# Fused dilated-window attention and squared-ReLU feed-forward: the second part of batch 0's plain values is loaded as f32 by SyncE and cast by VectorE, where GpSimd loaded and cast it before

## The chip, the cores and the metric

The kernel runs on one core of one Trainium2 chip. The number that counts is the device time of one execution in microseconds (us), the median of three runs. TensorE does the matrix products, ScalarE the exponentials, logarithms and most copies out of PSUM, VectorE the masks, products and other copies. GpSimd issues nearly all loads, because its DMAs can change f32 into bf16 on the way; SyncE issues the stores, the transposing DMAs and a few loads that change no type.

## The reference

Attention with a window of 32 keys over 8 batches, 8 heads, 576 tokens and 64 dimensions of a head. The first four heads ("plain") look at the last 32 tokens, the other four ("dilated") at every fourth of the last 128. Its result, as 4608 rows of 512, goes through a feed-forward layer with 2048 hidden columns and a squared ReLU.

```python
mask_plain = (rel >= 0) & (rel < window)                                    # rel = query - key, window = 32
mask_dil = (rel >= 0) & (rel < window * dilation) & (rel % dilation == 0)   # dilation = 4
scores = np.where(masks, scale * np.matmul(q, k.transpose(0, 1, 3, 2)), -1e9)
attn = np.exp(scores - np.max(scores, axis=-1, keepdims=True))
attn = attn / (np.sum(attn, axis=-1, keepdims=True) + 1e-09)
attn_out = np.matmul(attn, v)                                               # (8, 8, 576, 64)
x = attn_out.transpose(0, 2, 1, 3).reshape(4608, 512)
h = np.maximum(x @ w_in, 0.0)                                               # w_in (512, 2048)
out = h * h @ w_out                                                         # w_out (2048, 512)
```

## The kernel before

The order of everything is written by hand. A string PROGRAM lists short codes; a bar stands for one group of feed-forward matrix products. Codes that begin with L and a batch number are loads (`i0` to `i3` are the four column pieces of w_in, `o0` to `o3` the four row pieces of w_out, `v1p` the plain values of part two). For batch 0 the codes are a letter, a pair of heads e (0 and 1 plain, 2 and 3 dilated) and a part: T transposes q and k, C copies them out, S scores, E exponentials, P the product with the values, D the row sums, L and X the reciprocal, M the product into xT. Part one is the first 256 tokens of a batch, part two the other 320.

```python
PROGRAM = (
    "L0:q001 L0:q023 L0:q101 L0:q123 L0:v0d L0:i0 L0:v1dr L0:i1 L0:v1p L0:i2 L0:i3 L0:o0 L0:o1 L0:o2 L0:o3 "
    "L1:q00123 z y L1:v0dp L1:q10123 L1:v1dpr w9 T00 C00a ...  h W3 S20 E20 W2 S30 E30 T01 C01v ... P00 P10 D00 D10 L00 ..."
    "C31v W4 S01 S11 X00 M00 E01 E11 P20 P30 D20 D30 L20 X20 M20 S21 S31 W2+31 E21 E31 | | P21 P31 D21 D31 L21 "
    "X21 M21 L31 X31 M31 | | P01 P11 D01 D11 L01 X01 M01 L11 X11 M11 | | | ... "
    # ... (the rest: batches 1 to 7)
)
```

The values of the plain heads stand in `vbd[0]`, one 128 by 128 block for each pair of heads and 64 keys, with one head's values in the upper left and the other's in the lower right quarter. GpSimd loads those of part two (keys 256 to 575, five blocks) straight into it, four DMAs of 64 partitions, f32 in memory and bf16 in the tile:

```python
            if what == "p":                       # load_v; L0:v1p comes here with i0 = 4, i1 = 9
                for e in range(NE // 2):
                    for hl, rows in sides:
                        nc.gpsimd.dma_start(
                            dst[rows, e, i0:i1, rows],
                            v[b, 2 * e + hl, 64 * i0 : 64 * i1, :].rearrange("(i p) d -> p i d", p=64),
                        )
```

Part one takes another way: SyncE and ScalarE load it as f32 into a buffer of the output pool, which no output needs so early, and VectorE casts it into `vbd[0]` (code h):

```python
    osb_pool = ctx.enter_context(tc.tile_pool(name="osb", bufs=3))
    # ...
    plain = osb_pool.tile([P, DM], f32, name="osb")[:, :].rearrange("p (e i d) -> p e i d", e=2, d=D)
    nc.vector.tensor_copy(plain[:, :, 0, 0:1], mk[:, 0:2].unsqueeze(2))      # the loads wait for this copy
    for e, engine in enumerate((nc.sync, nc.scalar)):
        for hl, rows in enumerate(sides):
            engine.dma_start(
                plain[rows, e, :, :], v[0, 2 * e + hl, 0:256, :].rearrange("(i p) d -> p i d", p=64)
            )
    # ...
        elif code == "h":
            for rows in sides:
                nc.vector.tensor_copy(vbd[0][rows, 0:2, 0:4, rows], plain[rows, :, :, :])
```

The product with the values (P01 and P11 are part two of the plain pairs; each reads block 3 of part one first, then blocks 4 to 8), the product into xT (M), and the weights' load:

```python
        elif what == "P":      # first_step
            # ...
            for x, (i, r, q0, q1) in enumerate(bl):          # e 0 and 1, part two: blocks 3, 4 to 8
                # ...
                    lhs = vbd[0][:, e, i, :]
                    nc.tensor.matmul(to, lhs, rhs, start=(x == 0 and y0 == 0), stop=(x == len(bl) - 1), ...)   # line 595
        # ...
                nc.vector.tensor_tensor(out=to, in0=o, in1=rec, op=ALU.mult)                                   # M, line 628

    def load_w_in(x):          # line 776
        nc.gpsimd.dma_start(w_in_sb[x][:, :, :], moe_w_in[:, w_cuts[x] : w_cuts[x + 1]].rearrange("(kt p) f -> p kt f", p=P))
```

DMAs are counted on eight semaphores for GpSimd's and eight for the others', taken in turn. A DMA is issued once the one that used its semaphore eight DMAs earlier has landed.

The feed-forward products of the first 512 tokens run as two tiles of 256. Line 676 is the product with w_in, line 687 the ReLU on ScalarE, line 688 the square on VectorE, line 711 the product with w_out. An output tile of 128 tokens is copied out of PSUM and stored; in the last 512 tokens each store is cut into two halves of 256 columns:

```python
            if f1 == NF:       # g2
                osb = osb_pool.tile([P, DM], f32, name="osb")
                # ...
                nc.scalar.copy(osb[:, c0:mid], cur[m][:, c0:mid])                                             # line 718
                # ...
                for x in (c0, DM // 2) if c1 - c0 == DM and tk0 == NTOK - NT else (c0,):
                    store(osb, tk0 + P * m, x, DM // 2 if x < min(c1, DM // 2) and tk0 == NTOK - NT else c1)
```

Of the kernel before, what the change touches and what calls it, by code (L numbers as in the profile page):

```python
# [18 lines left out]


PROGRAM = (  # L21
    "L0:q001 L0:q023 L0:q101 L0:q123 L0:v0d L0:i0 L0:v1dr L0:i1 L0:v1p L0:i2 L0:i3 L0:o0 L0:o1 L0:o2 L0:o3 "
    "L1:q00123 z y L1:v0dp L1:q10123 L1:v1dpr w9 T00 C00a T10 C10a B00 B10 W2 S00 E00 B20 W1 S10 E10 u B30 W3 "
    "T20q W6 T20k C20v T30 C30v h W3 S20 E20 W2 S30 E30 T01 C01v T11 C11a P00 P10 D00 D10 L00 T21 C21v T31 "
    "C31v W4 S01 S11 X00 M00 E01 E11 P20 P30 D20 D30 L20 X20 M20 S21 S31 W2+31 E21 E31 | | P21 P31 D21 D31 L21 "
    "X21 M21 L31 X31 M31 | | P01 P11 D01 D11 L01 X01 M01 L11 X11 M11 | | | | | | | | | | | | | m n | | | | | "
    "L2:q00123 L2:q10123 | 1q1 1q3 | 1q2f 1k2f | 1k1a 1v3 | 1a2 | 1v2 1k0a 1q0v | 1o2 | 1a0 1a1 | 1k3 1o0 1o1f "
    "| 1a3 1Q0 | 1K0 1o3 | 1Q1 1K1 | 1Q2 | 1b0 | | 1Q3 1K2 L2:vwpdr L3:q00123 L3:q10123 | L2:x | | 2q0 | | 2k0 "
    "1V2 | 1b2 1p0 | 1b1 1V3 1K3 | | 1p2 1p1f | 2a0 1b3 | 2k1l 2o0 1p3f 2b0 2k1h | 2q1 2k2 L3:x | | 2q2 2p0 "
# [34 lines left out]
def kernel(  # L64
# [9 lines left out]
    nc = tc.nc  # L74
    P = nc.NUM_PARTITIONS
    B, H, S, D = q.shape
    DM, DFF = moe_w_in.shape
    NTOK = B * S
    assert H * D == DM
    bf16 = mybir.dt.bfloat16  # L80
    f32 = mybir.dt.float32
# [5 lines left out]
    NB = S // 64  # L87
# [5 lines left out]
    NT = 512  # L93
# [15 lines left out]
    osb_pool = ctx.enter_context(tc.tile_pool(name="osb", bufs=3))  # L109
# [23 lines left out]
    xT = const.tile([P, KT, RING], bf16, name="xT")  # L133
# [9 lines left out]
    vbd = [const.tile([P, NE, NB, P], bf16, name=f"vbd{i}") for i in range(2)]  # L143
# [6 lines left out]
    def staged(b: int, nm: str):  # L150


        t = rb[STAGE[b]][nm]
        return t[:, :].rearrange("p (a h x) -> p a h x", h=H, a=2)
# [309 lines left out]
    sides = [slice(64 * hl, 64 * hl + 64) for hl in range(2)]  # L464
# [175 lines left out]
    def store(osb, pos: int, c0: int = 0, c1: int = DM):  # L640

        x = 0
        while x < P:
            b, y = divmod(pos + x, S)
            part = int(y >= RES * MN[0]) if b in PARTED else 0
            w = MN[part] if b in PARTED else M
            r, m = divmod(y - RES * MS[part], w)
            n = min(P - x, w - m)
            row = b * S + RES * (MS[part] + m) + r
            nc.sync.dma_start(out[row : row + RES * (n - 1) + 1 : RES, c0:c1], osb[x : x + n, c0:c1])  # L650
            x += n

    def ffn_groups(tk0: int, nt: int):

        early = NT <= tk0 <= 2 * NT
        h2 = h2_pool.tile([P, NF, NT], bf16, name="h2T")
        per = NT // nt
        kts = (0, 2, 1, 3) if tk0 >= NT else (0, 1, 2, 3) if tk0 == 0 else (2, 3, 0, 1)  # L660
        cut = 3 if tk0 >= NT else 2
        cur, acc = {}, {}

        cuts = [(0, nt)] if tk0 // RING == (tk0 + nt - 1) // RING else [(0, -tk0 % RING), (-tk0 % RING, nt)]

        def mm1(u, ks):
            if u not in acc:
                acc[u] = ps_f.tile([P, NT], f32, name="pf")
            for x in range(per):
                f = per * u + x  # L670
                piece = max(y for y in range(len(w_in_sb)) if w_cuts[y] <= P * f)
                c0 = 512 * (f // 4) + f % 4 - w_cuts[piece]
                for kt in ks:
                    for y0, y1 in cuts:
                        t0 = (tk0 + y0) % RING
                        nc.tensor.matmul(  # L676
                            acc[u][:, nt * x + y0 : nt * x + y1],
                            w_in_sb[piece][:, kt, c0 : c0 + 509 : 4],
                            xT[:, kt, t0 : t0 + y1 - y0],
                            start=(kt == kts[0] and x == 0 and y0 == 0),  # L680
                            stop=(kt == kts[-1] and x == per - 1 and y1 == nt),
                            skip_group_check=True,
                        )
            if ks[-1] != kts[-1]:
                return
            hv = h2[:, per * u : per * u + per, 0:nt]
            nc.scalar.activation(hv, acc[u][:, :].rearrange("p (x n) -> p x n", x=per), ACT.Relu)  # L687
            nc.vector.tensor_tensor(out=hv, in0=hv, in1=hv, op=ALU.mult)  # L688

        def g1(i):  # L690
            if i < 2 and tk0 < NT:
                for u in range(2):
                    mm1(u, kts[2 * i : 2 * i + 2])
            elif i < 2 and early:
                for u in (2 * i, 2 * i + 1):
                    mm1(u, kts[:cut])
            elif i < 4 and early:
                for u in (2 * i - 4, 2 * i - 3):
                    mm1(u, kts[cut:])
            else:  # L700
                mm1(i, kts)

        def g2(m, part):
            last = tk0 + P * (m + 1) == NTOK
            if part == 0 or last and part == 2:
                cur[m] = ps_f.tile([P, DM], f32, name="pf")

            c0, c1 = (DM // 2 * (part // 2), DM // 2 * (part // 2 + 1)) if last else (0, DM)
            f0, f1 = (NF // 2 * (part % 2), NF // 2 * (part % 2 + 1)) if last else (4 * part, 4 * part + 4)
            for f in range(f0, f1):  # L710
                nc.tensor.matmul(  # L711
                    cur[m][:, c0:c1], h2[:, f, P * m : P * m + P], w_out_sb[:, f, c0:c1],
                    start=(f == 0), stop=(f == NF - 1),
                )
            if f1 == NF:
                osb = osb_pool.tile([P, DM], f32, name="osb")
                mid = (c0 + c1) // 2 if last else c1
                nc.scalar.copy(osb[:, c0:mid], cur[m][:, c0:mid])  # L718
                if last:
                    nc.vector.tensor_copy(osb[:, mid:c1], cur[m][:, mid:c1])  # L720
                for x in (c0, DM // 2) if c1 - c0 == DM and tk0 == NTOK - NT else (c0,):
                    store(osb, tk0 + P * m, x, DM // 2 if x < min(c1, DM // 2) and tk0 == NTOK - NT else c1)

        return [lambda i=i: g1(i) for i in range(NF // per)] + [
            lambda m=m, part=part: g2(m, part) for m in range(nt // P) for part in range(4)
        ]

# [3 lines left out]
    def zero_halves(t):  # L731
        nc.vector.memset(t[0:64, :, :, 64:128], 0.0)
        nc.vector.memset(t[64:128, :, :, 0:64], 0.0)
# [9 lines left out]
# [3 lines that stand above are left out]
                plain[rows, e, :, :], v[0, 2 * e + hl, 0:256, :].rearrange("(i p) d -> p i d", p=64)  # L746
            )
    near = mk[:, 0:96].rearrange("p (r m) -> p r m", r=RES)

    def put(dst, src):  # L750
        nc.scalar.copy(dst, src)
# [34 lines left out]
    def cross_all(b):  # L786
        for part in range(2):
            for nm in "kq":
                cross(b, nm, part)

    def run(code):
        if code == "y":
            for nm in "qk":
                nc.gpsimd.memset(staged(1, nm)[64:80, 0, :, :], 0.0)
                nc.gpsimd.memset(staged(2, nm)[64:80, 0, 0 : H // 2, :], 0.0)
        elif code == "z":
            nc.gpsimd.memset(vbd[1][0:64, :, :, 64:128], 0.0)
            nc.gpsimd.memset(vbd[1][64:128, :, :, 0:64], 0.0)
        elif code in "mu":
            masks(int(code == "u"))  # L800
        elif code == "h":
            for rows in sides:
                nc.vector.tensor_copy(vbd[0][rows, 0:2, 0:4, rows], plain[rows, :, :, :])
        elif code == "n":
            zero_halves(kbd)
            zero_halves(vbd[0][:, NE // 2 :, 0:8, :])
        elif code[0] in "wW":
            n, _, at = code[1:].partition("+")
            turn(int(n), 512 if code[0] == "w" else 256, [int(x) for x in at])
        elif code[0] in "TCBSEPDXM" or code[0] == "L" and code[2:3] != ":":  # L810
            first_step(code)
        elif code[0] != "L":
            step(int(code[0]), code[1:])
        else:
            b, what, part, which = int(code[1]), code[3], code[4:5], code[5:]
            if what == "q":
                load_qk(b, None if part == "w" else int(part), [int(e) for e in which])
            elif what == "x":
                cross_all(b)
            elif what == "v":  # L820
                load_v(b, [0, 1] if part == "w" else [int(part)], which)
            else:
                (load_w_in if what == "i" else load_w_out)(int(part))
# [22 lines left out]
    for code in program[0]:  # L846
        run(code)
# [43 lines left out]
```

The softmax here doesn't subtract the row's maximum and nothing guards it: scores larger than these inputs give would overflow.

## Time and profile before

| | |
|---|---|
| time, median of 3 runs | 309.02 us (308.62 to 309.26) |
| span of the profiled execution | 309.7 us |
| granted TensorE clock | 0.998 |
| TensorE products busy | 301.4 us, 97% of the span |
| ScalarE, VectorE busy | 198.2 us, 196.2 us |
| GpSimd busy | 93.8 us, nearly all before 195 us |
| DMA | 35.05 MB moved, mean 113 GB/s; the 16 DMA engines are busy at 70% or more in every slice up to 185 us |

The columns of the profile that are used below: in the chain of waits, start, length and what the time went to; in the timeline, start, length, engine, line, operation, output and inputs, count, and in brackets how long the engine sat idle before and what ended that; in the table by windows, for each engine the busy time and the number of instructions, then clock, mean busy share of the 16 DMA engines (it can pass 1, where packets overlap in time) and GB/s. The profiled execution is one run, so its 309.7 us stand beside the median of 309.02.

### The profile page before, as it was taken

The page shows a single profiled execution, that of the slowest core. Times are in us where ns is not written, and L with a number is a line of the kernel's source. Part 1 is how long each engine was busy: PE and PEld are TensorE (multiplying, and loading weights), DVE is VectorE, ACT ScalarE, POOL GpSimd, SP SyncE. Part 2 cuts the span into 40 slices and gives each one's busy share as a digit, 9 for nine tenths or more (in the row PEclk, how much of TensorE's full clock was granted, in tenths as well). Part 3 has the DMA queues.
Part 4 walks back from the last instruction along what each step waited for, and adds up shares of the span by engine and source line. Part 5 has one row for each costly group of instructions (what it writes and reads, how often), then busy time and mean ns, then how long its engine had stood idle before and what let it go on. Part 6 is the DMA issues. An engine that isn't in the chain of part 4 may idle for free.

```text
span 309.7 us, 6806 instructions
## 1 busy us (share of the span) xinstructions
PE 301.4 (97%) x2562; PEld 186.6 (60%) x2562; DVE 196.2 (63%) x645; ACT 198.2 (64%) x425; POOL 93.8 (30%) x138
## 2 busy tenths in 40 slices
PE   8898999999999999999999999999999999999995
PEld 3578856958855555555599555555555555445544
DVE  1555567888989889975798469946994334104400
ACT  7576748849977967795388547854686456216511
POOL 8489775546317345501551041000000000000000
PEclk9999999999999999999999999999999999999999
DMA  7999999999999979999799976502200210121022
GB/s 103 195 143 212 208 151 172 175 141 186 171 130 174 165 139 182 185 144 155 109 127 134 154 121 93 103 8 61 68 3 0 70 69 0 35 69 34 0 61 77
DMA packets 80288, 35.05 MB, mean 113 GB/s; under 512 B 49920, under 2 KB 75648, under 8 KB 80256
## 3 DMA queue, kind: packets, MB, share of 16 engines
q0 software_dynamic: 46592, 18.23, 52.4%
q1 hardware_dynamic: 32976, 16.06, 28.2%
q10 hardware_dynamic: 688, 0.33, 0.5%
q8 instruction: 20, 0.33, 0.4%
q14 instruction: 12, 0.10, 0.1%
HBM read 36.90 MB, written 9.44 MB: 150 GB/s over the span
## 4 chain that ended last, share of the span: by engine, by line
PE 81%; DMA 9%; ACT 3%; POOL 3%; issue 1%; DVE 1%; POOLq 0%; ACTq 0%
PE pf L711 38%; PE pf L676 35%; DMA w_in<-in_moe_w_in_dram 6%; DMA kb<-in_k_dram 4%; PE po L421 3%; PE pd L423 2%; PE pa L312 2%; PE pa L318 1%; POOL qb L161 1%; ACT h2T L687 1%; POOL kb L161 1%; PE pa L236 1%; ACT pt L322 1%; ACT qT L256 1%; ACT rec L425 0%
## 5 line engine op out<-in xcount | busy, mean ns | idle before, releaser
L676 PE MATMUL pf<-xT,w_in 128*128 128x256 bf16 (+1 forms) x768 | 133.5, 326 | 1.3 <-DMA w_in<-in_moe_w_in_dram 1.2
L711 PE MATMUL pf<-w_out_sb,h2T 128*128 128x512 bf16 (+1 forms) x592 | 134.2, 373 | 0.0
L676 PEld LDWEIGHTS <-w_in 128*128 128x128 bf16 x768 | 82.2, 114 | 36.6 <-DMA w_in<-in_moe_w_in_dram 1.8
L687 ACT ACTIVATE h2T<-pf 128x512 bf16<-128x512 f32 x144 | 83.8, 599 | 25.5 <-PE pf L676 24.8
L711 PEld LDWEIGHTS <-h2T 128*128 128x128 bf16 x592 | 54.3, 98 | 53.5
L688 DVE TENSOR_TENSOR h2T<-h2T 128x512 bf16<-128x512 bf16 x144 | 57.9, 422 | 40.2 <-ACT h2T L687 39.0
L718 ACT COPY osb<-pf 128x512 f32<-128x512 f32 (+1 forms) x37 | 21.0, 566 | 43.8 <-PE pf L711 35.8
L436 DVE TENSOR_TENSOR xT<-po,rec 128x288 bf16<-128x288 f32 (+2 forms) x51 | 23.2, 454 | 30.9 <-ACT rec L426 30.4
L178 POOL DMA_DIRECT2D vbd<-in_v_dram x36 | 25.7, 735 | 42.0 <-PE pd L423 37.2
L425 ACT ACTIVATE rec<-pd 128x288 f32<-128x288 f32 (+2 forms) x51 | 20.9, 411 | 20.4 <-PE pd L423 20.4
L322 ACT ACTIVATE pt<-pa 128x352 bf16<-128x352 f32 (+6 forms) x56 | 27.6, 499 | 7.1 <-PE pa L312 4.2
L426 ACT ACTIVATE rec<-rec 128x288 f32<-128x288 f32 (+2 forms) x56 | 24.8, 444 | 1.8
L421 PEld LDWEIGHTS <-vbd 128*128 128x128 bf16 x286 | 17.1, 97 | 9.4 <-issue 0.4
L256 DVE COPY qT<-xx 64x288 bf16<-64x288 bf16 x84 | 21.3, 253 | 1.1
L191 POOL DMA_DIRECT2D vd<-in_v_dram x24 | 14.7, 627 | 17.2 <-DMA kb<-in_k_dram 9.1
L161 POOL DMA_DIRECT2D qb<-in_q_dram x18 | 13.0, 720 | 16.7 <-DMA xx<-qb 15.1
L421 PE MATMUL po<-pt,vbd 128*128 128x32 bf16 (+3 forms) x256 | 17.5, 198 | 0.0
L260 DVE COPY kbd<-xx 64x288 bf16<-64x288 bf16 x36 | 17.0, 471 | 0.5
L423 PE MATMUL pd<-pt,mk 128*128 128x32 bf16 (+6 forms) x138 | 15.5, 203 | 0.0
L197 POOL DMA_DIRECT2D vbd<-in_v_dram x16 | 9.6, 602 | 14.6 <-PE pd L423 5.1
L161 POOL DMA_DIRECT2D kb<-in_k_dram x18 | 12.8, 711 | 0.8 <-DMA kb<-in_k_dram 0.5
L312 PE MATMUL pa<-qT,kbd 128*128 128x96 bf16 (+2 forms) x144 | 12.2, 202 | 0.0
(99 smaller groups left out, 240.3 us busy)
## 6 DMA issues: line engine op xcount, KB each, us to landing
out_dram<-osb SPq DMA_DIRECT2D x18, 128.0 KB, 3.4
qb<-in_q_dram POOLq DMA_DIRECT2D x7, 320.0 KB, 8.1
kb<-in_k_dram POOLq DMA_DIRECT2D x7, 320.0 KB, 10.4
vd<-in_v_dram POOLq DMA_DIRECT2D x32, 64.0 KB, 7.5
w_in<-in_moe_w_in_dram POOLq DMA_DIRECT2D x4, 512.0 KB, 8.0
w_out_sb<-in_moe_w_out_dram POOLq DMA_DIRECT2D x4, 512.0 KB, 13.0
qb<-in_q_dram POOLq DMA_DIRECT2D x7, 256.0 KB, 7.3
kb<-in_k_dram POOLq DMA_DIRECT2D x7, 256.0 KB, 8.1
```

What stands on the lines that cost most here:

```text
L161: nc.gpsimd.dma_start(t[0:n, part, hs, :], src[b, hs, t0 : t0 + RES * n, :].rearrange("h (p r) d -> p h (r d)", r=RES))
L178: nc.gpsimd.dma_start(dst[rows, e, i0:i1, rows], v[b, 2 * e + hl, 64 * i0 : 64 * i1, :].rearrange("(i p) d -> p i d", p=64),)
L256: copy(qT[rows, e, :, m0 : m0 + n].rearrange("p (c j) m -> p j c m", j=2)[:, jj, :, :], src)
L322: nc.scalar.activation(pt[:, off : off + n], ps[:, 0:n], ACT.Exp, scale=SCALE)
L421: nc.tensor.matmul(oo, vb[:, e, i, :], rh, start=(x == 0), stop=(x == len(mms) - 1), skip_group_check=True)
L423: nc.tensor.matmul(dd, ones[:, :], rh, start=(x == 0), stop=(x == len(dms) - 1), skip_group_check=True)
L426: nc.scalar.activation(rec[:, 0:n], rec[:, 0:n], ACT.Exp, scale=-1.0)
L436: nc.vector.tensor_tensor(out=tok, in0=o if o is o3 else o[:, 0:n], in1=rec if o is o3 else rec[:, 0:n], op=ALU.mult)
L676: nc.tensor.matmul(acc[u][:, nt * x + y0 : nt * x + y1], w_in_sb[piece][:, kt, c0 : c0 + 509 : 4], xT[:, kt, t0 : t0 + y1 - y0], start=(kt ...
L687: nc.scalar.activation(hv, acc[u][:, :].rearrange("p (x n) -> p x n", x=per), ACT.Relu)
L688: nc.vector.tensor_tensor(out=hv, in0=hv, in1=hv, op=ALU.mult)
L711: nc.tensor.matmul(cur[m][:, c0:c1], h2[:, f, P * m : P * m + P], w_out_sb[:, f, c0:c1], start=(f == 0), stop=(f == NF - 1),)
```

## The change

`L0:v1p` is gone: GpSimd no longer loads part two of the plain values, so what it issues behind (the weights i2, i3, o0 to o3, and batch 1) moves up by four DMAs. A new code `t` stands behind M20. For each of the two pairs it takes one more buffer of the output pool, writes one column of it from xT with VectorE (so that the load cannot be issued before that point of VectorE's program), and has SyncE load the f32 values into it, two DMAs for each pair. Codes `H0` and `H1`, behind M21 and M31, cast them into `vbd[0]` on VectorE. The three buffers of the output pool are all in use by then, one for part one and two for part two; the first stores come later. The purpose is to free GpSimd's queue of four small casting transfers in front of the weights, and to bring the weights sooner.

In the output, two more tiles of 128 tokens are stored in two halves, those of tokens 3840 to 4095. With the four new loads that makes eight more DMAs of SyncE in all, so each of the last stores keeps its turn among the eight semaphores.

```diff
-    "... L0:v0d L0:i0 L0:v1dr L0:i1 L0:v1p L0:i2 L0:i3 L0:o0 ..."
-    "... X20 M20 S21 S31 W2+31 E21 E31 | | P21 P31 D21 D31 L21 X21 M21 L31 X31 M31 | | P01 P11 ..."
+    "... L0:v0d L0:i0 L0:v1dr L0:i1 L0:i2 L0:i3 L0:o0 ..."
+    "... X20 M20 t S21 S31 W2+31 E21 E31 | | P21 P31 D21 D31 L21 X21 M21 H0 L31 X31 M31 H1 | | P01 P11 ..."
     (the lines of PROGRAM are cut here to what differs)
@@
-                for x in (c0, DM // 2) if c1 - c0 == DM and tk0 == NTOK - NT else (c0,):
-                    store(osb, tk0 + P * m, x, DM // 2 if x < min(c1, DM // 2) and tk0 == NTOK - NT else c1)
+                for x in (c0, DM // 2) if c1 - c0 == DM and tk0 + P * m >= NTOK - NT - 256 else (c0,):
+                    store(osb, tk0 + P * m, x, DM // 2 if x < min(c1, DM // 2) and tk0 + P * m >= NTOK - NT - 256 else c1)
@@
+    late = {}
@@
+        elif code == "t":
+            for e in range(2):
+                late[e] = osb_pool.tile([P, DM], f32, name="osb")[:, 0:320].rearrange("p (i d) -> p i d", d=D)
+                nc.vector.tensor_copy(late[e][:, 0, 0:1], xT[:, e, 0:1])
+                for hl, rows in enumerate(sides):
+                    nc.sync.dma_start(
+                        late[e][rows, :, :], v[0, 2 * e + hl, 256:S, :].rearrange("(i p) d -> p i d", p=64)
+                    )
+        elif code in ("H0", "H1"):
+            e = int(code[1])
+            for rows in sides:
+                nc.vector.tensor_copy(vbd[0][rows, e, 4:NB, rows], late[e][rows, :, :])
```

## The prediction

> **What bounds the kernel now.** I read the page's shares first: TensorE is busy 97% of the span, so a change in the loads can matter only where TensorE stands still. The list of waits names few such places, and one of them lies behind the loads that the change touches. The chain of waits, followed up to 30 us, shows it:
>
> ```profile
> 7.47 10.45 DMA w_in<-in_moe_w_in_dram
> 17.91 0.28 issue
> 18.20 1.30 POOL vbd L178 x2
> 19.50 6.79 DMA w_in<-in_moe_w_in_dram
> 26.29 0.05 issue
> 26.34 3.68 PE pf L676 x32
> ```
>
> The last two of GpSimd's four plain value DMAs (L178) stand in this chain: they wait until the first weight piece has landed at 17.91, and only behind them, at 19.50, is piece i2 issued. It lands at 26.29, and TensorE, which has nothing else to do, starts line 676 at 26.34. Next, what TensorE does just before, from its timeline:
>
> ```profile
> 23.21 0.39 PE L595 MATMUL po<-pt,vbd 128*128 128x32 bf16 x6
> 23.43 0.39 PE L595 MATMUL pa<-pt,vbd 128*128 128x32 bf16 x6
> 24.11 1.04 PE L676 MATMUL pf<-xT,w_in 128*128 128x256 bf16 x8
> 26.34 3.90 PE L676 MATMUL pf<-xT,w_in 128*128 128x256 bf16 x34 [1.19 <-DMA w_in<-in_moe_w_in_dram]
> ```
>
> The first two lines are P01 and P11, which read the values in question. They run at 23.2 with no wait. The wait for i2 is the 1.19 us in the bracket (1.5 by the weight loads). That is all there is to be won at this place. The table by windows shows why i2 is late, and what happens after:
>
> ```profile
> 18.00:20.00 2.00, 2.00 (x18) 1.66 (x19) 1.39 (x3) 1.56 (x4) 1.80 (x3) 1.00 1.52 163
> 20.00:22.00 2.00, 2.00 (x46) 1.74 (x46) 0.85 (x2) 1.35 (x4) 1.91 (x4) 1.00 0.80 49
> 22.00:24.00 2.00, 2.00 (x35) 1.99 (x34) 1.34 (x3) 1.97 (x5) 2.00 (x5) 1.00 1.16 182
> 26.00:64.00 38.00, 37.15 (x341) 27.86 (x341) 25.84 (x82) 26.65 (x67) 25.82 (x33) 1.00 1.25 180
> ```
>
> The last column is GB/s: it falls to 49 while the small value packets pass and no weights are queued behind them. The last line says that from 26 to 64 us TensorE stands still for 38.00 - 37.15 = 0.85 us only. So whatever is lost or won at 26 us travels on almost whole.
>
> **How such a load behaves.** Part one of the same values is already loaded by SyncE as f32; its tile answers what a load of this kind costs here:
>
> ```profile
> L745 SPq DMA_DIRECT2D osb<-in_v_dram x2: 770/798/827, 3.4 to 4.2; - x2
> L803 DVE CAST vbd<-osb x2: 421/422/424, 10.7 to 11.8; 64x512 bf16<-64x512 f32 x2
> L742 DVE CAST osb<-mk x1: 169/169/169, 3.2 to 3.2; 128x2 f32<-128x2 bf16 x1
> DMA to landing us min/median/max: 6.0/7.1/7.6
> ```
>
> An issue keeps SyncE 0.80 us, a cast of 64x512 takes 0.42 us, and from issue to landing it is 6.0 to 7.6 us beside GpSimd's queue, for DMAs of 64 KB. The quiet load of the masks at the start, 192 KB, takes 2.3 us.
>
> [...] in the packet records from 9 to 10 us, SyncE's queue moves 173 packets, ScalarE's 137 and GpSimd's 231, so no queue is shut out and none goes first. [...] for i2, 15 engines report by 25.16 and the last at 26.29.
>
> **The change part by part.** *Removed:* four DMA issues on GpSimd, 1.35 + 1.32 = 2.67 us, and 0.99 us of wait between them. i2 can then be issued where the first of them was, at 15.85 instead of 19.50, 3.65 us sooner, i3 right behind. Two 512 KB pieces at the 182 to 207 GB/s of the windows behind 22 us are 1049 KB / 0.2 = 5.2 us; with the first weights nearly done at 19, both should be in the tile at 24 or 25, and i2, which is first, before TensorE asks for it at 24.9. That takes the 1.2 us wait away.
>
> *Added on VectorE, before the loads:* M20 starts at 18.26 and takes 0.69 us, to 18.95; the first one-column copy at most 0.17, so SyncE issues its first load at about 19.1 and the others at 19.9, 20.7 and 21.5.
>
> *Added, the loads:* four DMAs of 64 partitions with five blocks, 320 packets of 256 bytes each, 1280 in all. They enter when i2, i3 and the w_out pieces fill GpSimd's queue. Estimate one: SyncE's first load of part one took 7.3 us to land with two other queues at work; with one rival less I take 5.7, so the first lands at 24.8. SyncE's two loads of 256 packets landed 1.15 us apart; 320 packets make 1.45, three more make 4.3: the fourth lands at 29.1. Estimate two: the first packet comes some 3 us after the issue (the store issued at 42.0 has its first packets at 45.0), at 22.1; 1280 packets at the 173 per us seen at 9 us take 7.4 us: 29.5. I take 29.3. The w_out pieces have packets of 4 KB of 323 ns, the w_in pieces of 1 KB of 98 ns, so turns get longer if the loads run into w_out: up to 33.
>
> *Added behind them:* the casts, 0.42 x 320/512 = 0.26 us each. P01 and P11 stand in TensorE's program before the products with i2 and now wait for the casts; that order is not changed. From the fourth landing it is one cast (0.26) and about 0.1 to hand over, the rest of P11 and the sums D01, D11 (23.43 to 24.11, 0.7), the eight products at 24.11 (0.9): 2.0 us. Line 676's long run begins at 29.3 + 2.0 = 31.3 instead of 26.34: 5.0 us later, in which the i2 wait is already accounted for. VectorE runs in order too: M31 stands behind H0 and two squares behind H1, but their readers are TensorE work behind the same wait.
>
> *Given back:* GpSimd and the loads run ahead of TensorE by then, so most of the 0.85 us that TensorE stands still from 26 to 64 us, above all 0.6 us for batch 2's k at 64.1, should go. I take 0.7 off. The eight more DMAs of SyncE, four of them stores near 280 us, cost nothing where SyncE mostly waits.
>
> Sum: 309.0 + 5.0 - 0.7 = 313.3 us.
>
> **The rivals.** *The aim comes true.* The f32 loads land before 24.3 (24.3 + 2.0 = 26.3 is the break-even), and up to 1.2 us are won: 307.8. For it: the loads are issued behind the weights' issue, and 320 KB are little. Against it: the last issue starts at 21.5, and from there even the 2.3 us of the quiet start give 23.8, while the DMA engines are at 182 GB/s and over. I give it one in ten.
> *Turns go well.* With all hardware queues' rate at 9 us, 173 + 137 = 310 packets per us, the fourth load is in at 22.1 + 4.1 = 26.2: the run starts 1.9 us late, 310.2 after the 0.7.
> *Turns go badly.* Landing at 33 in the midst of w_out makes 8.7 us late, 317.
>
> **Range and chances.** The three ways of landing set the range: 308.6 (between the aim and good turns) to 318.0 (bad turns and a late engine). 2% is 6.2 us, over 315.2: that needs the fourth load past 31.2, a quarter. Faster by over 2% would need 6 us at a place that holds 1.2: 0.02. The rest, 0.72, lies within 2%.
>
> **What would show it.** Right: TensorE waits at L595 for VectorE's cast at about 23, the cast for the f32 load; SyncE's loads take 6 us or more to land; no wait for w_in is left behind 18 us; the span up to 60 us is shifted by what L595 waited. Wrong: L595 at 23.2 with no wait, or a landing within 3 us of the issue; or a shift at 30 us that is gone by 64 us, which would say that TensorE's stretch has slack that its busy time hides.

## The result, and the profile after

The changed kernel takes 327.77 us, median of 4 runs (326.98 to 328.1), against 308.88 us (308.62 to 309.26) before: a ratio of 1.0607 [1.0584, 1.063]. The profiled execution has a span of 325.2 us. All but some 0.3 us of the loss arises before 53 us, at one place. The chain of waits of the changed kernel from 20.84 us on (start, length, what the time went to):

```profile
20.84 17.27 DMA osb<-in_v_dram
38.11 0.02 issue
38.13 0.49 DVE vbd L813
38.63 0.05 issue
38.67 0.55 PE pa L595 x5
...
40.03 12.31 PE pf L676 x96
```

Where the chain before went through GpSimd and a weight piece, it now goes through SyncE's fourth load of values: issued at 20.8, in the tile at 38.11, then the cast, then P11. TensorE's timeline at the same place:

```profile
22.60 0.18 PE L595 MATMUL po<-pt,vbd 128*128 128x32 bf16 x1
33.59 0.56 PE L595 MATMUL po<-pt,vbd 128*128 128x96 bf16 x5 [10.81 <-DVE vbd L813]
33.96 0.21 PE L595 MATMUL pa<-pt,vbd 128*128 128x32 bf16 x1
38.67 0.55 PE L595 MATMUL pa<-pt,vbd 128*128 128x96 bf16 x5 [4.50 <-DVE vbd L813]
...
39.84 12.50 PE L676 MATMUL pf<-xT,w_in 128*128 128x256 bf16 x96
```

P01 begins at 22.60 and, as before, with block 3, whose values are of part one. Its other five products need the new values: it waits 10.81 us, and P11, another pair, 4.50 us. The 96 products stand behind P11 in TensorE's program, and they start behind it, at 39.84, though the last piece of w_in has been in its tile since 26.42. The wait for w_in is gone: they run in one piece. VectorE's timeline says what the casts waited for:

```profile
27.30 0.48 DVE L813 CAST vbd<-osb 64x320 bf16<-64x320 f32 x1 [5.14 <-DMA osb<-in_v_dram]
33.05 0.48 DVE L813 CAST vbd<-osb 64x320 bf16<-64x320 f32 x1 [5.28 <-DMA osb<-in_v_dram]
...
36.96 0.48 DVE L813 CAST vbd<-osb 64x320 bf16<-64x320 f32 x1 [2.90 <-DMA osb<-in_v_dram]
38.13 0.48 DVE L813 CAST vbd<-osb 64x320 bf16<-64x320 f32 x1 [0.69 <-DMA osb<-in_v_dram]
```

Each starts when its own load lands. The tile's own view, from 13 to 45 us:

```profile
L807 SPq DMA_DIRECT2D osb<-in_v_dram x4: 601/633/1071, 18.4 to 20.8; - x4
...
DMA to landing us min/median/max: 8.8/15.4/17.3
```

Loads of 80 KB are up to 17.3 us on their way. The DMA engines are not short of work meanwhile, as the table by windows shows (in each row the busy time of TensorE comes second, the granted clock third from the end, GB/s last):

```profile
26.00:30.00 4.00, 0.00 (x0) 0.00 (x0) 0.48 (x1) 0.00 (x0) 4.00 (x4) 0.57 1.08 210
30.00:34.00 4.00, 0.41 (x6) 0.41 (x6) 0.92 (x2) 0.00 (x0) 3.13 (x5) 0.50 1.07 209
...
42.00:44.00 2.00, 2.00 (x13) 1.50 (x12) 0.00 (x0) 0.52 (x1) 2.00 (x4) 0.58 1.28 170
```

They move 210 GB/s, nearly all of it w_out pieces, which nobody reads before line 711 starts, at 52 us here and at 36 before. And there is a second thing in this table: the clock of the idle TensorE falls to 0.50 and is still there when the work resumes at 38.67 (it is back at 1.00 at 43.66). Which queue got the bandwidth can be counted from the packet records of the trace, by queue and microsecond (a count of the records, not a view of the profile):

| us | GpSimd's queue | SyncE's queue |
|---|---|---|
| 23 | 147 of 1 KB (i3), 96 ns each | 154 of 256 B |
| 26 to 33 | 47 to 49 of 4 KB (w_out), 322 ns each | 44 to 59 of 256 B, 30 ns each |
| 35, 36 | 167, 243 of 512 B (queries) | 178, 199 of 256 B |

While both have work, the two queues move about the same number of packets, at each of the three sizes. 16 engines with one pair of 322 + 30 = 352 ns each would make 16 / 0.352 = 45 pairs per us; the table has a little more, since the records overlap in time: the starts of the 4 KB packets lie 331 ns apart, less than 352.

### The profile page after: what moved, and what is told of

It is laid out like the page before. It is cut to its first block, busy times and chain, and to the rows that moved or that the text cites. A ratio compares the mean times of both kernels' runs of the same rounds, so it can differ in the third digit from the quotient of the medians.

```text
span 325.2 us, 6794 instructions
## 1 busy us (share of the span) xinstructions
PE 302.2 (93%) x2530; PEld 188.5 (58%) x2562; DVE 197.9 (61%) x651; ACT 198.4 (61%) x425; POOL 91.2 (28%) x134
## 4 chain that ended last, share of the span: by engine, by line
PE 86%; DMA 7%; ACT 2%; issue 1%; DVE 1%; POOL 1%; SPq 0%; ACTq 0%; POOLq 0%
PE pf L676 38%; PE pf L711 37%; DMA osb<-in_v_dram 5%; PE po L421 3%; PE pd L423 2%; DMA kb<-in_k_dram 2%; PE pa L312 2%; PE pa L318 1%; PE pa L236 1%; POOL qb L161 1%; ACT h2T L687 1%; PE pa L505 0%; POOL kb L161 0%; ACT pt L565 0%; PE pf L421 0%
## 5 line engine op out<-in xcount | busy, mean ns | idle before, releaser
L711 PE MATMUL pf<-w_out_sb,h2T 128*128 128x512 bf16 (+1 forms) x570 | 131.0, 373 | 1.2
L676 PEld LDWEIGHTS <-w_in 128*128 128x128 bf16 x768 | 83.1, 114 | 36.3 <-issue 0.4
L178 POOL DMA_DIRECT2D vbd<-in_v_dram x32 | 23.0, 738 | 68.4 <-PE pd L423 62.1
L256 DVE COPY qT<-xx 64x288 bf16<-64x288 bf16 x84 | 20.3, 241 | 1.1
L421 PE MATMUL po<-pt,vbd 128*128 128x32 bf16 (+3 forms) x256 | 17.6, 199 | 0.0
L197 POOL DMA_DIRECT2D vbd<-in_v_dram x16 | 9.7, 616 | 10.8 <-PE pd L423 7.1
```

Source lines behind the costliest of these rows:

```text
L178: nc.gpsimd.dma_start(dst[rows, e, i0:i1, rows], v[b, 2 * e + hl, 64 * i0 : 64 * i1, :].rearrange("(i p) d -> p i d", p=64),)
L421: nc.tensor.matmul(oo, vb[:, e, i, :], rh, start=(x == 0), stop=(x == len(mms) - 1), skip_group_check=True)
L676: nc.tensor.matmul(acc[u][:, nt * x + y0 : nt * x + y1], w_in_sb[piece][:, kt, c0 : c0 + 509 : 4], xT[:, kt, t0 : t0 + y1 - y0], start=(kt ...
L711: nc.tensor.matmul(cur[m][:, c0:c1], h2[:, f, P * m : P * m + P], w_out_sb[:, f, c0:c1], start=(f == 0), stop=(f == NF - 1),)
```

## The experiments

The theory to test, A: SyncE's packets take turns one for one with GpSimd's, so next to 4 KB packets they crawl, TensorE waits for the fourth load, and its clock falls on top. The rival B: the loads are slow for a reason of their own (latency, the number of loads, the total bandwidth), and the size of the other queue's packets does not matter. The second question: what was there to be won at all, had the values been in time?

To read all runs with one measure, each is told by its 96 products at line 676 that stand behind P11: their start, their length (10.65 us at full clock in a profile with nothing in between), and their end. A ratio is formed from those executions alone that lie within 1.5% of the fastest of their kernel, so it need not be the quotient of the medians beside it.

**e1, no loads.** It leaves out the loading of part two's values: the casts stay where they are and read part one's buffer.

```diff
-    late = {}
+    late = plain.rearrange("p e i d -> p (e i) d")[:, 0:5, :]
         elif code == "t":
-            (the loop with two buffers, two copies and four SyncE loads)
+            pass
-                nc.vector.tensor_copy(vbd[0][rows, e, 4:NB, rows], late[e][rows, :, :])
+                nc.vector.tensor_copy(vbd[0][rows, e, 4:NB, rows], late[rows, :, :])
```

> This kernel leaves the loading of part two's plain values out: the casts H0 and H1 stand where they stood and read part one's buffer, so TensorE gets other numbers. It shows what the removal from GpSimd's queue brings if the values cost no transfer. Theory A (all of the loss is the wait for SyncE's loads, and the clock behind it): no wait at L595, the wait for w_in piece i2 gone, 307.5 us, between 306.8 and 308.9. Rival (the earlier weights or the six VectorE instructions cost something by themselves): 310 us or more.

Measured: 311.21 us against 309.64, ratio 1.0063 [1.0038, 1.0087]. Of the loss of 6.1% only 0.6% is left, so the loads made nearly all of it. But nothing is won either: the time is the rival's, 310 us or more. VectorE:

```profile
22.62 0.98 DVE L807 CAST vbd<-osb 64x320 bf16<-64x320 f32 x2
23.64 0.49 DVE L628 TENSOR_TENSOR xT<-pa,rec 128x320 bf16<-128x320 f32 x1
24.05 0.98 DVE L807 CAST vbd<-osb 64x320 bf16<-64x320 f32 x2
```

Two of the casts stand behind M31 (L628), and are done at 25.03. TensorE waits for them:

```profile
25.08 0.37 PE L595 MATMUL pa<-pt,vbd 128*128 128x96 bf16 x5 [1.03 <-DVE vbd L807]
25.74 10.65 PE L676 MATMUL pf<-xT,w_in 128*128 128x256 bf16 x96
```

The new wait of 1.03 us has taken the place of the wait for i2. Casts of 0.48 us each are on the path even without a transfer.

**e2, w_out in 1 KB packets.** Each w_out piece is loaded by two DMAs whose packets are 1 KB and not 4 KB; the bytes are the same.

```diff
-        nc.gpsimd.dma_start(
-            w_out_sb[:, 4 * c : 4 * c + 4, :].rearrange("p f m -> p (f m)"),
-            moe_w_out[512 * c : 512 * c + 512, :].rearrange("(p f) m -> p (f m)", p=P),
-        )
+        for y in range(2):
+            nc.gpsimd.dma_start(
+                w_out_sb[:, 4 * c + y : 4 * c + 4 : 2, :],
+                moe_w_out[512 * c : 512 * c + 512, :].rearrange("(p a b) m -> p a b m", p=P, b=2)[:, :, y, :],
+            )
```

> The changed kernel with w_out loaded in packets of 1 KB instead of 4 KB (two DMAs for each piece, every other row). Theory A (each DMA engine takes one packet from each queue in turn, so SyncE's 256-byte packets move at the pace of the packet next to them): SyncE's rate stays near 150 packets per us instead of 50, its fourth load lands at about 31 us instead of 38.1, and the time falls by about 7 us to 320.5 (318 to 322). Rival B (SyncE's queue is slow by itself, whatever stands beside it): the fourth load lands at about 38 us, the time stays at 327.8 within 1 us.

Measured: 322.17 us, ratio 1.0393 [1.0341, 1.0444]. TensorE's waits:

```profile
PE po L595 <- DVE vbd L814: 6.2, 1, 6.2
PE pa L595 <- DVE vbd L814: 3.6, 1, 3.6
```

9.8 us of waiting in place of 15.3, at about the same GB/s (193 from 26 to 30 us, against 210). The packet records from 24 to 30 us show 143 to 155 packets of 1 KB beside 137 to 161 of 256 B in each microsecond: one for one again, three times as many. The fourth load lands at 32.90 and not at 38.11 (about 31 was expected, and 318 to 322 us). That is A, and B is out: only the form in which the other queue loads w_out had changed.

**e3, TensorE kept busy.** 90 idle products ahead of P01 and 38 ahead of P11, on a tile of no meaning, into a buffer that nobody reads.

```diff
-    "... M31 H1 | | P01 P11 D01 ..."
+    "... M31 H1 | | Y90 P01 Y38 P11 D01 ..."
+        elif code[0] == "Y":
+            warm = ps_f.tile([P, 512], f32, name="pf")
+            for _ in range(int(code[1:])):
+                nc.tensor.matmul(warm[:, 0:256], idle[:, 0:P], idle[:, :], start=True, stop=True, skip_group_check=True)
```

> The changed kernel with 90 idle products of 256 columns in front of P01 and 38 in front of P11, in the time in which TensorE waits; they should end before the casts do. Theory C (of the loss some 2.5 us is the halved TensorE clock behind the wait, on top of the wait itself): the granted clock stays near 1.0 behind the wait and the time falls by 2.0 to 3.0 us to about 325.2. Rival (the clock row does not matter to the time): 327.8 us within 0.5.

Measured: 326.03 us, ratio 1.0509 [1.045, 1.0568]. TensorE:

```profile
40.57 0.39 PE L595 MATMUL pa<-pt,vbd 128*128 128x32 bf16 x6
41.24 10.65 PE L676 MATMUL pf<-xT,w_in 128*128 128x256 bf16 x96
```

The clock is 1.00 in every window from 26 to 42 us, and the 96 products take 10.65 us in place of 12.50: the halved clock costs 1.85 us there. The median falls by 1.7 us, from 327.77 to 326.03, where 2.0 to 3.0 were expected. The two profiled spans differ by only 0.3 us. In the profiled execution of e3 the clock was halved earlier, from 14.10 to 17.52, and the first product with w_in came at 18.41 instead of 17.05. So the loads were issued from 19.63 on and not from 18.39, the fourth landed at 39.67, the last idle products ended after its cast, and the 96 products start 1.4 us later than in the changed kernel.

**e4, the loads 7 us earlier.** Code t right behind h, its one-column copies from the mask tile.

```diff
-    "T20k C20v T30 C30v h W3 ... X20 M20 t S21 ..."
+    "T20k C20v T30 C30v h t W3 ... X20 M20 S21 ..."
-                nc.vector.tensor_copy(late[e][:, 0, 0:1], xT[:, e, 0:1])
+                nc.vector.tensor_copy(late[e][:, 0, 0:1], mk[:, 0:1])
```

> The changed kernel with the four f32 loads issued at about 12.3 us, behind the cast of part one (code h), their one-column copies reading the mask tile instead of xT. Beside them GpSimd's queue then has packets of 512 bytes and 1 KB, none of 4 KB. Theory A (one packet in turn): 150 packets per us or more from about 15 us, fourth load landed at 23.5 us, TensorE hardly waits at L595; the first weights come up to 1.5 us later; 309 us, between 307.5 and 311. Rival B (SyncE's queue is slow by itself, some 70 packets per us): landing at 33 us, about 320 us.

Measured: 310.98 us, ratio 1.0052 [1.0035, 1.007]. The loads are issued from 11.8 to 13.7, before the w_out pieces, and the fourth lands at 22.94, ahead of its cast. What is left:

```profile
PE pf L676 <- DMA w_in<-in_moe_w_in_dram: 0.8, 1, 0.8
PE pa L595 <- DVE vbd L813: 0.6, 1, 0.6
```

The first line is i1, which shares the DMA engines with the loads now (it lands at 22.11, in the kernel before, e0 below, at 20.92); the second the casts, as in e1. Earlier loads take away the loss of the change, and the gain does not come.

**e5, the store split alone.** The kernel before with the two cut stores, nothing else.

```diff
-                for x in (c0, DM // 2) if c1 - c0 == DM and tk0 == NTOK - NT else (c0,):
+                for x in (c0, DM // 2) if c1 - c0 == DM and tk0 + P * m >= NTOK - NT - 256 else (c0,):
     (and the same condition in the line behind it)
```

> The kernel before with only the other part of the change: tokens 3840 to 4095 stored in halves. Theory A (those stores lie beside TensorE's products near 280 us and cost nothing): the time of the kernel before, within 0.3%. Rival (they shift the last stores): slower by 0.5 us or more. Its profile is also a second look at how long the kernel before waits for w_in piece i2.

Measured: 310.82 us against 309.28, ratio 1.0042 [1.0026, 1.0058]. From the last ReLU to the end it is 17.60 us, against 17.33 in the kernel before; the same 17.6 are in e1 and e10, which have the cut stores but not the four loads, while the changed kernel and e4, with all eight more DMAs, have 17.33. So the cut costs 0.28 us where the loads are missing, and nothing in the change itself. The expectation, within 0.3%, was missed all the same. In e5's profile the span is 1.6 us longer than that of e0 (the kernel before once more, below), and 0.9 of them arise before 36 us, where the two programs are alike: i2 is waited for 1.15 us here, against 0.51 in e0. Why was not found, nor where the rest comes from.

**e6, early loads, casts ahead of M21.** e4, with H0 and H1 moved ahead of the last two normalizations, and the casts written with an even number of parts (two halves of 32 columns).

```diff
-    "... P31 D21 D31 L21 X21 M21 H0 L31 X31 M31 H1 | | P01 ..."
+    "... P31 D21 D31 H0 H1 L21 X21 M21 L31 X31 M31 | | P01 ..."
-                nc.vector.tensor_copy(vbd[0][rows, e, 4:NB, rows], late[e][rows, :, :])
+                nc.vector.tensor_copy(
+                    vbd[0][rows, e, 4:NB, rows].rearrange("p i (y d) -> p y i d", y=2),
+                    late[e][rows, :, :].rearrange("p i (y d) -> p y i d", y=2),
+                )
```

> e4 with two edits: the casts H0 and H1 stand in front of M21 (VectorE has idle time there) and run over an even outer dimension (two halves of 32 columns instead of five blocks). Theory A (in e4 what is left is 0.6 us of waiting for the casts, which stand in VectorE's chain behind M21, and 0.8 us for w_in piece i1, which shares its turns with SyncE's loads): no wait at L595, a cast takes about 0.32 us instead of 0.48, 0.6 us less than e4, so the time of the kernel before within 0.3%. Rival (the order of the casts does not matter): e4's time, 0.5% over the kernel before.

Measured: 314.8 us, ratio 1.0139 [1.0105, 1.0173]; missed. The casts:

```profile
20.24 0.31 DVE L813 CAST vbd<-osb 64x320 bf16<-64x320 f32 x1
21.22 0.32 DVE L813 CAST vbd<-osb 64x320 bf16<-64x320 f32 x1 [0.67 <-DMA osb<-in_v_dram]
23.11 1.70 DVE L813 CAST vbd<-osb 64x320 bf16<-64x320 f32 x1 [1.57 <-DMA osb<-in_v_dram]
25.09 1.86 DVE L813 CAST vbd<-osb 64x320 bf16<-64x320 f32 x1 [0.28 <-DMA osb<-in_v_dram]
```

The even form takes 0.31 us in place of 0.48, until GpSimd clears the next batch's value buffer:

```profile
22.59 2.04 POOL L798 MEMSET vbd<- 64x2304 bf16 x1
24.67 2.10 POOL L799 MEMSET vbd<- 64x2304 bf16 x1
```

The third and the fourth cast each end 0.18 us after a memset does (24.81 after 24.63, 26.95 after 26.77). The first two, at 20.24 and 21.22, ran before any memset. So beside a memset a cast of the even form took 1.70 and 1.86 us here; how the one holds up the other the traces do not show. In five blocks a cast beside a memset keeps its 0.48 us (e9, below).

**e7, no loads, casts ahead of M21, even form.** e1 with the order and the form of e6; it leaves out the loading, too.

```diff
-    "... P31 D21 D31 L21 X21 M21 H0 L31 X31 M31 H1 | | P01 ..."
+    "... P31 D21 D31 H0 H1 L21 X21 M21 L31 X31 M31 | | P01 ..."
-                nc.vector.tensor_copy(vbd[0][rows, e, 4:NB, rows], late[rows, :, :])
+                (the same in the even form, as in e6)
```

> e1 (part two's plain values are not loaded; the casts read part one's buffer) with the casts in front of M21 and over an even outer dimension. Theory A (e1 gained nothing because four casts of 0.48 us behind M21 took the place of the wait for i2): no wait at L595 and none for i2, 0.4 to 0.6% under the kernel before, about 1.5 us under e1. Rival (something else in the earlier weights costs the time in e1): e1's time, 0.6% over the kernel before.

Measured: 315.68 us, ratio 1.0141 [1.0097, 1.0185]; missed. With no load to wait for, the casts are held up as well:

```profile
19.91 5.56 DVE L807 CAST vbd<-osb 64x320 bf16<-64x320 f32 x4
```

Four casts take 5.56 us, 0.31 the shortest and 2.72 the longest, beside memsets from 21.10 to 25.28, and M21 comes behind them: TensorE waits 3.92 us for xT. So e6's loss isn't one of late loads alone.

**e8, two of the four loads on ScalarE.**

```diff
-                    nc.sync.dma_start(
+                    (nc.sync, nc.scalar)[e].dma_start(
```

> The changed kernel with the second pair's two f32 loads issued by ScalarE instead of SyncE. Theory A (one packet from each queue in turn): beside w_out's 4 KB packets SyncE's and ScalarE's queues move 45 to 50 packets per us each, so the last of the four loads lands at about 32 us instead of 38 and the time is 5 to 7 us less than the changed kernel's 327.8. Rival (all loads that are not GpSimd's share a fixed rate of 50 packets per us): landing at 38 us, 327.8 us within 1.

Measured: 324.14 us, ratio 1.049 [1.0459, 1.0522]. In the packet records at 26 us the three queues stand at 43 (GpSimd, 4 KB), 53 and 56 packets per us: one for one for one. The loads' two queues move 109 of these 152 packets, and the last loads land at 32.6 and not at 38.1. TensorE's waits:

```profile
PE po L595 <- DVE vbd L813: 7.2, 1, 7.2
PE po L595 <- DVE pt L568: 2.1, 1, 2.1
PE pa L595 <- DVE vbd L813: 0.8, 1, 0.8
```

8.0 us for the casts in place of 15.3, and 2.1 us new: ScalarE issues two DMAs for 1.86 us ahead of the exponentials that make pt. The landing is A's once more. The time fell by 3.6 us, not by the 5 to 7 expected: behind the 2.1 us the clock was halved from 22.70 on, and 16 products at 22.44 took 3.37 us in place of 1.94.

**e0, the kernel before once more**, with a comment line added (its line numbers are one higher).

```diff
+# the kernel before, unchanged
```

> The kernel before, unchanged but for a comment: what two equal programs differ by, and a second profile of it. Expected: ratio 1.000 within 0.3%, a wait of about 1.1 us for w_in piece i2 at line 676.

Measured: 309.36 us in 22 runs, ratio 0.9986 [0.9968, 1.0004]. Its profile has a span of 307.6 us, where the profile read for the prediction has 309.7:

```profile
17.00 1.04 PE L677 MATMUL pf<-xT,w_in 128*128 128x256 bf16 x8
...
22.97 0.39 PE L596 MATMUL pa<-pt,vbd 128*128 128x32 bf16 x6
23.64 1.04 PE L677 MATMUL pf<-xT,w_in 128*128 128x256 bf16 x8
25.19 9.80 PE L677 MATMUL pf<-xT,w_in 128*128 128x256 bf16 x88 [0.51 <-DMA w_in<-in_moe_w_in_dram]
```

The wait for i2 is 0.51 us here, not 1.19. It varies between executions, and half a microsecond is what the change could have taken away in this one. The two profiled executions took 309.37 us (e0) and 311.46: the second, from which the prediction was read, lies 2.4 us above the median of 309.02.

**e9, e6 with the casts of five blocks** (0.48 us each, the form of the change).

```diff
     (e6, with its cast written as in the changed kernel)
+                nc.vector.tensor_copy(vbd[0][rows, e, 4:NB, rows], late[e][rows, :, :])
```

> e6 with the casts in the form of the change, five blocks of 64 columns, so that only their place in front of M21 differs from e4. Theory A (the casts of e6 over an even outer dimension stood still while GpSimd filled its tiles with zeros, and those over five blocks do not): each cast 0.48 us, M21 not held up, 0.6 us under e4: the time of the kernel before within 0.3%. Rival (casts in front of M21 are held up in any form): 1.4% over the kernel before, as e6.

Measured: 312.1 us, ratio 1.0089 [1.0065, 1.0114]. The profiled execution is one of the longest, 314.76 us:

```profile
24.06 0.48 DVE L813 CAST vbd<-osb 64x320 bf16<-64x320 f32 x1 [1.76 <-DMA osb<-in_v_dram]
26.07 0.48 DVE L813 CAST vbd<-osb 64x320 bf16<-64x320 f32 x1 [1.53 <-DMA osb<-in_v_dram]
26.58 0.49 DVE L628 TENSOR_TENSOR xT<-po,rec 128x320 bf16<-128x320 f32 x1
```

No cast is stretched now, though memsets of 2.0 us run from 22.69 to 26.78, and the time is still lost: VectorE waits for the third and fourth load (they land at 23.97 and 26.05), and M21, which stands behind their casts in its program, starts at 26.58. The expectation was half right.

**e10, e1 with the casts ahead of M21 in five blocks**; it leaves out the loading. This is the best case of the idea: no transfer, casts that no memset holds up, in VectorE's idle time.

```diff
-    "... P31 D21 D31 L21 X21 M21 H0 L31 X31 M31 H1 | | P01 ..."
+    "... P31 D21 D31 H0 H1 L21 X21 M21 L31 X31 M31 | | P01 ..."
     (otherwise e1)
```

> e7 (no loading of part two's plain values) with the casts over five blocks. Theory A: each cast 0.48 us instead of the 5.56 us of the four in e7, no wait at L595 and none for i2: 0.3 to 0.5% under the kernel before, the most that the idea can bring. Rival: 1.4% over the kernel before, as e7.

Measured: 309.77 us against 309.44, ratio 1.0004 [0.9985, 1.0023]; 0.3 to 0.5% under the kernel before were expected.

```profile
21.03 2.01 DVE L807 CAST vbd<-osb 64x320 bf16<-64x320 f32 x4
23.08 0.49 DVE L628 TENSOR_TENSOR xT<-po,rec 128x320 bf16<-128x320 f32 x1
```

```profile
17.74 1.04 PE L676 MATMUL pf<-xT,w_in 128*128 128x256 bf16 x8
```

No wait for w_in is left, but 2.01 us of casts stand ahead of M21, and TensorE waits 0.41 us for it. From the first product with w_in, at 17.74, to the end of the 96 products at 35.16 it is 17.42 us, against 17.99 in e0 (17.00 to 34.99), 18.30 in e5 and 18.17 in the first profile of the kernel before; so 0.6 us or a little more is won at the place. It is not seen in the time: this execution came to the first product 0.74 us later than e0, and 0.28 us are the tail of e5. Even free values bring nothing that the time shows, and no run beats the kernel before.

**All runs by one measure.** Start and length of the 96 products come from TensorE's timeline of each run. For e0 the two groups of 8 and 88 are taken together, ending at 25.19 + 9.80 = 34.99; likewise for the first profile of the kernel before and for e5, where the length holds the wait for i2.

| run | start, us | length, us | end behind e0's, us | span minus 307.6, us |
|---|---|---|---|---|
| kernel before, first profile | 24.11 | 12.02 | 1.14 | 2.1 |
| e5 store split | 23.88 | 11.98 | 0.87 | 1.6 |
| changed kernel | 39.84 | 12.50 | 17.35 | 17.6 |
| e1 no loads | 25.74 | 10.65 | 1.40 | 1.9 |
| e2 1 KB packets | 34.63 | 12.82 | 12.46 | 12.7 |
| e3 TensorE busy | 41.24 | 10.65 | 16.90 | 17.3 |
| e4 early loads | 25.62 | 10.65 | 1.28 | 1.3 |
| e6 early casts, even | 28.41 | 10.65 | 4.07 | 4.9 |
| e7 no loads, early, even | 27.61 | 12.44 | 5.06 | 5.6 |
| e8 two queues | 35.59 | 12.69 | 13.29 | 13.5 |
| e9 early casts, five | 28.70 | 11.53 | 5.24 | 5.4 |
| e10 no loads, early, five | 24.51 | 10.65 | 0.17 | 0.6 |

In the ten changed kernels the last two columns agree to within 0.9 us, in seven of them to within 0.5: what is lost by 53 us is nearly the loss of the whole kernel, and hardly any of it is given back behind. The first two rows say how far two profiles differ by themselves: one is the same program as e0, the other the same but for stores at its end, and their ends lie 1.1 and 0.9 us behind. So for ends about as far apart as that, those of e1, e4 and e10, the medians decide and not this table.

## Why the prediction was wrong

- **The place and the wait: right.** TensorE waits at L595 for the casts, the casts for SyncE's loads, the loads take far more than 6 us, the wait for w_in behind 18 us is gone, and the shift travels to the end.
- **The landing: the term that failed.** The fourth load was put at 29.3 us, and 33 as the worst; it landed at 38.11, 8.8 us later. The start was right (first packets at 22.29 us, 22.1 in estimate two), with some luck: the issue came 0.7 us earlier than thought, at 18.39, and the first packet 3.9 us behind it and not 3. Both estimates then took a rate seen next to small packets: 173 packets per us at 9 us. Next to w_out's 4 KB packets it is 44 to 59, beside 47 to 49 of those. The 323 ns, and turns that get longer beside them, were in the text; the rate was not worked out from them. Taking one packet of each in turn, 16 / 0.352 = 45 per us was to be had beforehand as an estimate. As counted, 397 of the 1280 packets pass by 26 us, 484 in the nine microseconds beside w_out, and the last 399 in little more than two behind it.
- **Behind the landing: small.** From the fourth landing to the 96 products it was 39.84 - 38.11 = 1.7 us, against 1.1 (the 2.0 of the text without the 0.9 of the eight products, which are now among the 96). A cast took 0.48 us, not 0.26: the scaling from the 64x512 cast did not hold. The rest of P11 and the sums ran at half the clock (38.67 to 39.84, 1.17 us, against 0.7).
- **The clock: missing.** The text had no term for it. The clock fell to 0.50 while TensorE waited, and the 96 products took 12.50 us in place of 10.65 (e3, where TensorE was kept busy and the clock stayed at 1.00): 1.85 us.
- **The base: mis-sized.** The 26.34 was read from an execution of 311.46 us whose wait for i2 was 1.19 us, while the sum was started from the median of 309.0. In e0, at 309.37, the same products start at 25.19, 1.15 us sooner.
- **Given back, 0.7: right for that execution alone.** Behind the 96 products it takes 273.55 us to the end of the span, the changed kernel 272.85. In e0, where TensorE does not wait for batch 2's k, it is 272.57, so there was nothing to give back: the lag against e0 is 17.35 us at 52 us and 17.6 at the end.

The account closes. Against the profile that was read, the end of the 96 products moves from 36.13 to 52.34, 16.2 us: 5.0 (predicted) + 8.8 (landing) + 0.6 (behind it) + 1.85 (clock) = 16.25. Against e0 it is 4.3 (predicted) + 8.8 + 0.6 + 1.85 + 1.15 (base) + 0.7 (not given back) = 17.4 us, with 17.6 between the two spans. The medians of the times are 18.9 apart.

Of the rivals, "turns go badly" named the right danger with too small a size; its packet of 4 KB was the cause. "The aim comes true" could not have won its 1.2 us: e10 has the aim without any transfer, wins about 0.6 us at the place in its profile, and stands at 1.0004.

What stays open: what e5 loses beside its tail; and how much of the shorter waits in e8 would be left if SyncE alone issued on two queues, which wasn't tried.

## What to carry to other kernels

Before a small load is moved to another queue, ask what that queue's packets will alternate with. Here 16 engines, divided by the time of one own packet plus one of each other queue, gave a fair estimate of its rate, somewhat low (45 per us for 44 to 59 counted; 127, from 16 / 0.126 us, for 137 to 161 in e2). In the changed kernel a load of 256-byte packets, with nothing else in its own queue, moved 44 to 59 of them per us beside a weight stream of 4 KB packets, where 173 per us had passed in the kernel before beside packets of 256 and 512 bytes. A load that TensorE waits for belongs ahead of a bulk stream that nobody waits for (e4: 1.0052 in place of 1.0607), or in the same queue ahead of it, as the kernel before had it. And before any of that, read the wait to be won in a second profile: here it was 1.19, 0.51 and 1.15 us in three, and the new way added four casts of 0.48 us.

## What was not expected of the hardware

**One packet each, at every size met here.** In the packet records each queue moves about as many rows of its DMAs as the other: 47 to 49 rows of 4 KB stand against 44 to 59 of 256 B, 149 of 1 KB against 152 (e2), and with three queues 43 : 53 : 56 (e8). Counts by the microsecond could also come from long batches on engines out of step, but the starts of the rows leave no room for that. With the queue alone (e1 and the kernel before, 28 to 34 us) most rows of 4 KB are followed by another start 305 ns later; beside one queue of small rows (changed kernel, 27 to 34 us) it is 331 ns, for the small rows too, beside two (e8, 26 to 29 us) 345. For rows of 1 KB (e2) it is 78 ns alone and 105 beside one. So these starts fit one small row between each two large ones, and 16 / 0.331 makes the 48 per us of the table.

**The clock was halved for multiples of 3.41 us.** From the mean clock of windows of 1 us, the moment of a step can be worked out: in the changed kernel these are

```profile
26.00:27.00 1.00, 0.00 (x0) 0.00 (x0) 0.00 (x0) 0.00 (x0) 1.00 (x1) 0.80 1.08 206
...
43.00:44.00 1.00, 1.00 (x9) 0.79 (x7) 0.00 (x0) 0.52 (x1) 1.00 (x2) 0.67 1.18 152
```

0.80 is 0.6 us at 1.00 and 0.4 at 0.50, so the clock fell at 26.60, 3.8 us after TensorE's last product, and it rose at 43.66, 5.0 us after work resumed. The halved stretches of six runs, worked out so:

| run | halved from, to, us | length, us |
|---|---|---|
| changed kernel | 26.60, 43.66 | 17.06 = 5 x 3.41 |
| e2 | 25.44, 39.10 | 13.66 = 4 x 3.41 |
| e3 | 14.10, 17.52 | 3.42 |
| e7 | 24.48, 31.30 | 6.82 = 2 x 3.41 |
| e8 | 22.70, 26.12; 29.54, 39.78 | 3.42; 10.24 = 3 x 3.41 |
| e9 | 27.10, 30.52 | 3.42 |

All are multiples of 3.41 us, and the stretch at full clock between the two of e8, from 26.12 to 29.54, is one too. The same idle time may or may not cost: e6 and e7 both wait 3.92 us, and only e7's clock fell (e6 has 1.00 from 18 to 34 us). In e9 it fell at the end of a wait of 2.55 us, and in e3 at 14.10, where the longest wait just before was 1.12 us. What makes the clock fall at one wait and not at another these runs do not show.

**A faster form of a cast can be the slower one.** In e6 and e9 a cast of 64x320 took 0.31 us alone and up to 1.86 beside a GpSimd memset, against 0.48 in five blocks both alone and beside it.
